# One decode step with attention over a cache: where the last rows of W_up lie, how wq is transferred, and which queue brings the first K tile

## The chip, the core and the metric

The kernel runs on one core of a Trainium2 chip. The core has a matrix engine (TensorE, PE), a vector engine (VectorE, DVE), a scalar engine (ScalarE, ACT), a general engine (GpSimd, POOL) and an engine that here only issues transfers (SyncE, SP). Transfers from memory are issued by SP and by ScalarE, each on a queue of its own (q1 and q10 in the profile), and are carried out by the core's 16 DMA engines. Data lies in SBUF (128 partitions); matrix products land in PSUM. The metric is the device time of one execution in microseconds (us); lower is better.

## The reference

One token goes through two branches that a sigmoid gate mixes. Branch a is attention of 16 query heads over 8 cached key and value heads of 65536 positions; branch b is a small gated network.

```python
g = _sigmoid((x * gate_w).sum(-1, keepdims=True))
a = _A_ref(x, A_k_cache, A_v_cache, A_wq, A_wo)   # q = x @ wq; softmax(q k^T / 16) v; @ wo
b = _B_ref(x, B_W_gate, B_W_up, B_W_down)         # (relu(x W_gate) * (x W_up)) @ W_down
return g * a + (1 - g) * b
```

Everything is bf16. x has 448 elements, wq is 448 x 4096, wo 4096 x 448, W_gate and W_up are 448 x 1792, W_down is 1792 x 448. The caches are 8 x 65536 x 256 each, 268 MB each, and each is read once.

## The kernel before

K and V stream through a ring of three SBUF buffers, `ring[0..2]`, each of 128 partitions x 64 KB. A tile of K or V (4 for each of the 8 heads, 32 of each) fills one buffer. A list `order` (lines 228 to 244) fixes the order of the tiles and of wo's two parts on SP's queue and assigns each tile the next buffer in turn; `held` and `freed` (lines 254 to 259) say which operations must have read a buffer before the next tile may be issued into it. For a K tile DVE transposes the buffer in place in 32 x 32 blocks (line 454), PE forms the scores (`f_qk`), DVE takes their maximum and ScalarE the exponential. When all four tiles of a head are done, the weights are rescaled and V tiles are multiplied (`make_pv`).

Every operation is entered into a plan with an engine, a key (its place in that engine's order, no time) and the operations it depends on. `_Plan.finish` sorts each engine's operations by key and puts semaphore waits where a dependency needs one; `mop` marks the operations on the shared PSUM bank `M_ps`, and `serialize` puts these one behind another in the order of keys.

The start is the part that the change touches. The buffers `ring[1]` and `ring[2]` first hold weights, and `ring[0]` gets the first K tile, K0.

- ScalarE issues W_gate's first 384 rows (3 rows to a partition), x, gate_w, W_gate's last 64 rows as half rows on 128 partitions (`wfh[0]`), and W_up's first 384 rows (lines 271 to 277).
- SP issues wq's first 384 rows (`wq3`, one transfer of 128 partitions, into `ring[2]`), wq's last 64 rows (`wqa`, into `ring[1]`), W_up's last 64 rows as half rows (`wfh[1]`), K0, then W_down, which waits for the query projection because it overwrites `wq3`, and then K1 into `ring[1]`, which waits for the query projection as well (`held[1]` is `["q"]`). K2 goes into `ring[2]` and waits for the gate, up and down products.
- When x is there, POOL spreads its last 64 elements (`f_xp`), PE turns x into columns (`f_xT`), DVE copies them to `xT` and lays them out for the query projection (`f_xw`). The sigmoid of the gate is computed along the way (`z0` to `z7`, over POOL, DVE, ScalarE and PE).
- PE then runs the query projection (`f_q`, 48 matmuls in a loop; `f_q2`, 16), the gate and up products (`f_gu` over 384 rows, 24 matmuls; `f_gu2` over the last 64 rows, 8), and, when DVE has formed h (lines 656 to 660), the down product (`f_dn`).

In a loop made by `step`, the addresses are held in registers of PE's sequencer, which are moved on in each turn. `raw_mm` takes a matmul with or without a load of its weights; `same_weights` is a matmul that uses the weights loaded before it. A matmul of one output row uses 32 columns of the array, so four stand side by side in four column groups.

At the end, wo for heads 0 to 3 and the rest of wo come behind the V tiles, and the products of PE's `f_wo` add up in the PSUM bank `A_ps`, into which the down product has gone already.

Of the kernel before, what the change touches and what calls it, by code (L numbers as in the profile page):

```python
# [9 lines left out]
U32 = mybir.dt.uint32  # L10
# [15 lines left out]
class _Plan:  # L26
# [8 lines left out]
    def op(self, eng, key, fn, deps=(), incs=1, split=False):  # L35
        o = _Op(eng, key, fn, deps, incs=incs, split=split)
        self.ops.append(o)
        return o

    def dma(self, eng, key, sem, fn, deps=()):  # L40
        if sem not in self.dsem:
            self.dsem[sem] = self.es.enter_context(self.nc.semaphore("d_" + sem))
        o = _Op(eng, key, fn, deps, dma=sem)
        self.ops.append(o)
        return o
# [66 lines left out]
def bass_gated_mix__gqa_block_cached__glu_gated_reglu__decode_kernel(  # L112
# [25 lines left out]
    NR3 = R3 * 128  # L138
    HD = D // 2
    NW = R3 + 2  # L140
    NX = R3 + 2
    FT = F // 128
    SCALE = 1.0 / 16.0
    NEGBIG = -3.0e38
# [7 lines left out]
    with es:  # L152
# [40 lines left out]
        g_row = P2[1][:, 1024:1024 + 2 * FW].bitcast(F32)  # L193
        h_row = P2[1][:, 0:FW]

        wq3 = ring[2][:, 0:R3 * NQ]
        wqa = ring[1][:, 0:NQ // 2]
        WB = R3 * NQ
        wf3 = [ring[2][:, WB + i * R3 * F:WB + (i + 1) * R3 * F] for i in range(2)]
        WB += 2 * R3 * F  # L200
        wfh = [ring[2][:, WB + i * (F // 2):WB + (i + 1) * (F // 2)] for i in range(2)]
        assert WB + F <= U * DH and FW * 4 == F and FW <= 512
        wd_sb = ring[2][:, 0:FT * D].rearrange("p (ft d) -> p ft d", ft=FT)

        ST = [ps("ST%d" % i, [128, 512], F32) for i in range(2)]
# [45 lines left out]
        T_END = t + 20.0  # L251


        slot, held, freed = {}, {1: ["q"], 2: ["gu", "dn"]}, {}
        r = 0
        for kind, i, _ in order:
            if kind in ("k", "v"):
# [6 lines left out]
        for key, (kind, i, _) in home.items():  # L264
# [7 lines left out]
            wf3[0], B_W_gate[0:NR3, :].rearrange("(p k) f -> p (k f)", k=R3)))  # L272
        d_x = dma("ac", -9, "x", lambda e: e.dma_start(x_row, A_x[0, :, :]))
        d_gw = dma("ac", -8, "gw", lambda e: e.dma_start(gw_row, gate_w.rearrange("(o d) -> o d", o=1)))
        half = lambda i, W: lambda e: e.dma_start(wfh[i], W[NR3:D, :].rearrange("r (c f) -> (r c) f", c=2))
        d_wh0 = dma("ac", -7, "wfh0", half(0, B_W_gate))
        d_wu = dma("ac", -6, "wf1", lambda e: e.dma_start(
            wf3[1], B_W_up[0:NR3, :].rearrange("(p k) f -> p (k f)", k=R3)))

        c_xp = op("gp", -0.3, lambda e: e.memset(x_per, 0.0))  # L280
        c_o1 = op("gp", -0.2, lambda e: e.memset(one_t[:], 1.0))
        c_nil = op("gp", -0.1, lambda e: e.memset(nil_t[:], 0.0))
# [37 lines left out]
        def f_xT(e):  # L320
            for kt in range(R3):
                e.matmul(XT_ps[:, kt:kt + 1], x_row[0:1, kt:NR3:R3], one_t[0:1, 0:1], start=True, stop=True)
            for kt in range(NX - R3):
                ins = e.matmul(XT_ps[:, R3 + kt:R3 + kt + 1], x_per[0:1, kt * 128:kt * 128 + 128], one_t[0:1, 0:1], start=True, stop=True)  # L324
            return ins

        def f_xp(e):
            xr = x_row[0:1, NR3:D]
            for c in range(2):
                ins = e.tensor_copy(x_per[0:1, 129 * c:129 * c + 127:2], xr)  # L330
            return ins
        x0_ = op("gp", 0.97, f_xp, [d_x, c_xp])
        x1_ = mop("pe", 0.98, f_xT, [d_x, c_o1, x0_])

        def f_xT2(e):
            return e.tensor_copy(xT[:], XT_ps)  # L336
        x2_ = mop("dv", 0.985, f_xT2, [x1_])
        g_em = op("dv", 2.1, lambda e: e.tensor_reduce(
            emat[:], identb[:].rearrange("p (y r) -> p r y", r=8)[:, 0:4, :], AX.X, ALU.max), [g_idb])
# [67 lines left out]
        def step(e, ws, vs, dw, dv, count, mms):  # L407
            rw, rv = pr[0:len(ws)], pr[len(ws):len(ws) + len(vs)]
            w0 = at(ws[0], True)

            def body():
                e.reg_alu(rw[0], rw[0], dw, ALU.add)
                adds(e, (rw[0], ws[0], True), [(r_, w, True) for r_, w in zip(rw[1:], ws[1:])])
                e.reg_alu(rv[0], rv[0], dv, ALU.add)
                adds(e, (rv[0], vs[0]), [(r_, v, False) for r_, v in zip(rv[1:], vs[1:])])
                for o, i, j, pos, size in mms:
                    ins = raw_mm(e, o, via(ws[i], rw[i]), via(vs[j], rv[j]), pos, True, size)
                return ins
            v0 = at(vs[0])
            return rolled(e, [(rw[0], w0 - dw), (rv[0], v0 - dv)], rv[0], v0 + (count - 1) * dv, body)  # L420
# [190 lines left out]

        for kind, i, t in issue:
            if kind == "wq":
                l_["wq"] = dma("sp", t, "wq", lambda e: e.dma_start(wq3, A_wq[0:NR3, :].rearrange("(p k) n -> p (k n)", k=R3)))
                l_["wqh"] = dma("sp", t + 0.01, "wqh", lambda e: e.dma_start(
                    wqa, A_wq[NR3:D, :].rearrange("r (c n) -> (r c) n", c=2)))
                d_wh1 = dma("sp", t + 0.02, "wfh1", half(1, B_W_up))
                tq = tL["wq", 0]
                l_["qm"] = mop("pe", tq, f_q, [l_["wq"], q0, c_nil, g_idb], incs=J)
                l_["q"] = mop("pe", tq + 8, f_q2, [l_["qm"], l_["wqh"]], incs=J // 2)  # L620
# [5 lines left out]
            elif kind == "gu":  # L626
                t = tL["gu", 0]
                a1 = [d_wg, d_wu]
                a2 = [d_wh0, d_wh1]

                def f_gu(e):
                    for kt in range(R3):
                        for i_ in range(2):
                            for w in range(4):
                                o, v = OP[i_][32 * w:32 * w + 1, 0:FW], wf3[i_][:, kt * F + w * FW:kt * F + (w + 1) * FW]
                                if i_ == 0:
                                    ins = e.matmul(o, xT[:, kt:kt + 1], v, start=(kt == 0), stop=False, skip_group_check=True,
                                                   tile_position=(0, 32 * w))
                                else:
                                    ins = same_weights(e, o, xT[:, kt:kt + 1], v, kt == 0, (0, 32 * w))  # L640
                    return ins

                def f_gu2(e):
                    for w in range(4):
                        for i_ in range(2):
                            o, v = OP[i_][32 * w:32 * w + 1, 0:FW], wfh[i_][:, w % 2 * FW:(w % 2 + 1) * FW]
                            x = xT[:, R3 + w // 2:R3 + w // 2 + 1]
                            if i_ == 0:
                                e.matmul(o, x, v, start=False, stop=False, skip_group_check=True, tile_position=(0, 32 * w))
                            else:  # L650
                                ins = same_weights(e, o, x, v, False, (0, 32 * w))
                    return ins
                tg, tr0 = tL["k", 0] - 6.6, tL["k", 0] - 0.5
                l_["gm"] = op("pe", tL["gu", 0] + 3, f_gu, a1 + [x2_, c_ps[3]])
                l_["gu"] = op("pe", tr0, f_gu2, a2 + [l_["gm"]])
                l_["relu"] = op("dv", tr0 + 0.1, lambda e: e.tensor_scalar_max(g_row, OP[0][:, 0:FW], 0.0), [l_["gu"], z1, l_["xm"]])
                l_["h"] = op("dv", tr0 + 0.2, lambda e: e.scalar_tensor_tensor(
                    h_row.rearrange("p (t q) -> p q t", q=32), g_row.rearrange("p (q t) -> p q t", q=32), gb[:, 1:2],
                    OP[1][:, 0:FW].rearrange("p (q t) -> p q t", q=32), ALU.mult, ALU.mult), [l_["relu"], z7])
                l_["hT"] = op("dv", tr0 + 0.3, lambda e: e.transpose(h_row, h_row), [l_["h"]])  # L660
            elif kind == "wd":
                a3 = dma("sp", t, "wd", lambda e: e.dma_start(wd_sb, B_W_down.rearrange("(p ft) d -> p ft d", ft=FT)), [l_["q"]])

                def f_dn(e):
                    f_nil(e, [A_ps])
# [3 lines left out]
            elif kind == "k":  # L669
                n = i  # L670
                h, t_ = divmod(n, NTH)
                sl = slot["k", n]
                kd = dma("sp", t, "r%d" % sl, lambda e, n=n, sl=sl: e.dma_start(ring[sl][:], k_src(n)), free(("k", n)))
# [89 lines left out]

        t7 = last["tn", H - 1]
        for i in range(len(WOP)):
            for k, (h, lo, hi) in enumerate(WOP[i]):
                key = tL["wo", i] + 0.01 * k
                if i == 1:
                    key = t7 + (-0.3 if h < NP else 0.6) + 0.01 * k
                wv = wo_sb[:, h:h + 2, :, :].rearrange("p h s n -> p (h s) n") if h < NP else wo_sb[:, h, :, :]  # L770

                def f_wo(e, h=h, lo=lo, hi=hi, wv=wv, end=(i == 1 and k == len(WOP[i]) - 1), roll=(i == 0)):
                    if roll:
                        return step(e, [attnT[:, h * 4 + lo:h * 4 + lo + 1]], [wv[:, lo, g * HD:(g + 1) * HD] for g in range(2)], 2, 2 * D, hi - lo,
                                    [(A_ps[32 * g:32 * g + 1, 0:HD], 0, g, (0, 32 * g), (128, 32)) for g in range(2)])
                    for s in range(lo, hi):
                        for g in range(2):
                            c = h * 4 + s
                            ins = e.matmul(A_ps[32 * g:32 * g + 1, 0:HD], attnT[:, c:c + 1], wv[:, s, g * HD:(g + 1) * HD],
                                           start=False, stop=(end and s == hi - 1), skip_group_check=True,  # L780
                                           tile_position=(0, 32 * g))
                    return ins
                fin = op("pe", key, f_wo, [l_["wo", h, lo], last["norm", h], last["norm", h + 1] if h < NP else None], incs=hi - lo if i == 0 else 1)
        f1 = [op(("dv", "ac")[g], T_END, lambda e, g=g: (e.copy if g else e.tensor_copy)(
            fin_o[:, g * HD:(g + 1) * HD], A_ps[32 * g:32 * g + 1, 0:HD]), [fin]) for g in range(2)]
        f2 = dma("ac", T_END + 1, "out", lambda e: e.dma_start(
# [38 lines left out]
```

## Time and profile before

| | us |
|---|---|
| median of three runs | 1275.67 (1275.54 to 1275.78) |
| the profiled execution | 1275.64 |
| its span, from the first to the last instruction | 1274.2 |
| DVE busy | 648.7 (51% of the span) |
| PE busy | 371.4 (29%) |
| ScalarE busy | 58.2 (5%) |
| POOL busy | 37.2 (3%) |
| moved by the DMA engines | 549.20 MB, 431 GB/s in the mean |

A row of the timeline reads: start in us from the beginning of the span, duration in us, engine, line of the kernel, operation, the tile written and the tiles read, their sizes, and how many instructions were merged into the row; in brackets the idle time of that engine before it and what ended it. SPq and ACTq are the issuing of transfers by those engines. A row of the table by stretches gives the stretch, its length, each engine's busy time and (in brackets) its instructions, the granted PE clock as a share of full speed, the mean busy share of the 16 DMA engines and the rate in GB/s. Transfers are counted where their packets start, so that in stretches of a few us a share can exceed 1. A DMA queue's row gives packets, MB, and the time of its packets as a share of 16 engines over the span.

### The profile page before, as it was taken

What the parts mean: (1) busy time and instruction counts of PE and PEld (TensorE: products, weight loads), DVE (VectorE), ACT (ScalarE), POOL (GpSimd) and SP (SyncE); (2) the same over time, 40 slices, a digit from 0 to 9 for tenths busy, and PEclk for the clock granted to TensorE, in tenths of its full rate; (3) what the DMA queues carried; (4) which work ended last, traced back from release to release, by engine and by line L of the source; (5) the groups of instructions that cost most, each with busy time, mean ns of one, the idle gap of its engine ahead of it and who ended that gap; (6) DMA issues with size and microseconds to landing.
All of it is one profiled execution on the core that took longest, in us unless ns stands there. A gap on an engine that the chain in (4) does not pass through costs nothing.

```text
span 1274.2 us, 9555 instructions
## 1 busy us (share of the span) xinstructions
PE 371.4 (29%) x4483; PEld 105.0 (8%) x2909; DVE 648.7 (51%) x171; ACT 58.2 (5%) x112; POOL 37.2 (3%) x94
## 2 busy tenths in 40 slices
PE   4413222323133331224220342311332203223154
PEld 2101000101000000001000010000100000000010
DVE  1797633566534655445555454556535565336511
ACT  0000000000000000000000000000000000000000
POOL 2000000000000100001000010000100001000010
PEclk9566666656666665665656676556766556666577
DMA  9999999999999999999999999999999999999998
GB/s 414 429 444 428 426 428 430 447 438 428 428 432 428 442 435 434 428 434 428 441 434 434 428 434 430 439 434 434 428 438 428 436 434 434 430 438 428 436 421 378
DMA packets 11522, 549.20 MB, mean 431 GB/s; under 512 B 1267, under 2 KB 1654, under 8 KB 2422
## 3 DMA queue, kind: packets, MB, share of 16 engines
q1 hardware_dynamic: 11072, 546.05, 99.2%
q10 hardware_dynamic: 438, 2.98, 0.6%
q8 instruction: 8, 0.13, 0.0%
q14 instruction: 4, 0.03, 0.0%
HBM read 549.03 MB, written 0.00 MB: 431 GB/s over the span
## 4 chain that ended last, share of the span: by engine, by line
DMA 42%; DVE 32%; PE 16%; another core or an unknown queue 7%; issue 1%; POOL 0%; ACT 0%; SPq 0%; ACTq 0%
DMA ring<-in_A_k_cache_dram 34%; DVE ring L454 27%; PE ST L373 9%; PE O L373 5%; DMA ring<-in_A_v_cache_dram 4%; DMA ring<-in_A_wo_dram 3%; DVE P L701 1%; DVE P L699 1%; PE M_ps L373 1%; DVE o_sb L497 1%; DMA P<-in_A_x_dram 1%; DVE nmb L680 1%; PE ST L403 0%; PE M_ps L694 0%
## 5 line engine op out<-in xcount | busy, mean ns | idle before, releaser
L454 DVE STREAM_TRANSPOSE ring<-ring 128x16384 uint32<-128x16384 uint32 (+1 forms) x36 | 552.3, 15345 | 318.9 <-DMA ring<-in_A_k_cache_dram 318.9
L403 PE MATMUL ST<-nil_t,identb 1*128 1x1 bf16 x32 | 5.1, 158 | 767.6 <-DVE ring L454 767.6
L373 PE MATMUL ST<-ring,xm 128*16 x2048 | 185.2, 537 | 4.6 <-issue 0.7
L373 PE MATMUL O<-ring,P 128*32 x2016 | 133.9, 425 | 20.8 <-DMA ring<-in_A_v_cache_dram 18.3
L680 DVE TENSOR_REDUCE nmb<-ST 128x1 f32<-128x512 f32 x32 | 22.0, 688 | 185.0 <-PE ST L373 185.0
L682 ACT ACTIVATE P<-ST,nmb 128x512 bf16<-128x512 f32 x32 | 45.2, 1413 | 1082.8 <-DVE nmb L680 1082.8
L373 PEld LDWEIGHTS ST<-ring,xm 128*16 x2048 | 61.5, 112 | 115.2 <-issue 101.5
L403 PEld LDWEIGHTS ST<-nil_t,identb 1*128 1x128 bf16 x32 | 3.2, 100 | 792.6 <-issue 792.6
L497 DVE CAST_PREDICATED o_sb<-bm,O 128x512 bf16<-128x512 uint16 (+1 forms) x33 | 22.3, 679 | 69.2 <-PE O L356 46.9
L690 POOL TENSOR_TENSOR hs<-selc,hs 128x2 f32<-128x2 f32 x8 | 1.6, 196 | 1143.7 <-DVE hs L688 1143.7
L373 PEld LDWEIGHTS O<-ring,P 128*32 x504 | 15.7, 113 | 112.9 <-issue 110.4
L699 DVE TENSOR_TENSOR P<-P,hs 128x2048 bf16<-128x2048 bf16 x8 | 18.3, 2292 | 8.1 <-ACT hs L696 8.1
L702 POOL TENSOR_TENSOR hs<-hs,rs 128x4 f32<-128x4 f32 x8 | 18.4, 2305 | 13.6 <-ACT hs L696 13.6
L701 DVE STREAM_TRANSPOSE P<-P 128x2048 bf16<-128x2048 bf16 x8 | 18.5, 2311 | 0.3
L707 PE MATMUL M_ps<-hs,ones_f 128*128 128x2 f32 x16 | 4.7, 364 | 30.3 <-POOL hs L706 30.3
L373 PE MATMUL M_ps<-ring,P 128*128 x64 | 13.0, 341 | 1.5 <-PE M_ps L373 0.3
L525 PE MATMUL M_ps<-emat,o_sb 128*64 128x2 bf16 x48 | 3.0, 185 | 22.0 <-ACT o_sb L507 22.0
L682 ACT ACTIVATION_READ_ACCUMULATOR P<-ST,nmb 128x1 f32 x32 | 8.4, 263 | 0.0
L373 PEld LDWEIGHTS M_ps<-ring,P 128*128 x64 | 7.5, 119 | 6.9 <-issue 5.3
L336 DVE CAST xT<-M_ps 128x5 bf16<-128x5 f32 x1 | 0.2, 167 | 14.7 <-PE M_ps L324 14.7
L622 DVE STREAM_TRANSPOSE P<-P 128x128 uint32<-128x128 uint32 x1 | 0.3, 311 | 12.7 <-ACT P L621 12.7
L707 PEld LDWEIGHTS M_ps<-hs,ones_f 128*128 128x128 f32 x16 | 4.0, 312 | 30.9 <-POOL hs L706 30.9
(103 smaller groups left out, 94.0 us busy)
## 6 DMA issues: line engine op xcount, KB each, us to landing
ring<-in_A_v_cache_dram SPq DMA_DIRECT2D x3, 4096.0 KB, 28.9
ring<-in_A_v_cache_dram SPq DMA_DIRECT2D x2, 2048.0 KB, 36.3
ring<-in_A_wq_dram SPq DMA_DIRECT2D x1, 3072.0 KB, 13.2
ring<-in_A_wo_dram SPq DMA_DIRECT2D x1, 1792.0 KB, 19.6
ring<-in_B_W_down_dram SPq DMA_DIRECT2D x1, 1568.0 KB, 10.1
ring<-in_B_W_gate_dram ACTq DMA_DIRECT2D x1, 1344.0 KB, 13.4
ring<-in_B_W_up_dram ACTq DMA_DIRECT2D x1, 1344.0 KB, 26.5
ring<-in_A_wo_dram SPq DMA_DIRECT2D x1, 896.0 KB, 40.3
```

The costliest lines, as they stand in the source:

```text
L373: return e.add_instruction(mybir.InstMatmult(name=nc.get_next_instruction_name(), engine=e.engine, ins=[v, w], outs=[e.lower_ap(o)], start ...
L403: e.matmul(o, identb[0:1, :], nil_t[0:1, 0:1], start=True, stop=False, skip_group_check=True)
L454: return lambda e: e.transpose(v, v)
L497: return e.copy_predicated(dst, m.to_broadcast(list(src.shape)), src)
L525: ins = e.matmul(T_ps[p0:p0 + 64, s:c1 + 1:c1 - s], t[:, c:c + 64], emat2[:], start=(s == 0), stop=False, skip_group_check=True, tile_posi ...
L680: smax[n] = op("dv", tk + 26, lambda e, n=n, NM=NM, t_=t_: e.tensor_reduce(NM[:, t_:t_ + 1], ST[n % 2][:], AX.X, ALU.max, negate=True), [q ...
L682: aexp[n] = op("ac", tk + 27, lambda e, n=n, t_=t_, NM=NM, RS=RS, Ph=Ph: e.activation(Ph[:, t_:2048:4], ST[n % 2][:], ACTF.Exp, bias=NM[:, ...
L690: h2 = op("gp", T + 13.55, lambda e, X=X: e.tensor_tensor(X[:, 2:4], selc[:, 2:4], X[:, 0:1].to_broadcast([128, 2]), ALU.mult), [h1, g_sel])
L699: rsc = op("dv", T + 16, lambda e, X=X, pb=pb: e.tensor_tensor(pb, pb, X[:, 12:16].unsqueeze(1).to_broadcast([128, 512, 4]), ALU.mult), [h ...
L701: last["ev", h] = [op("dv", T + 17, lambda e, Ph=Ph: e.transpose(Ph[:], Ph[:]), [rsc])]
L702: l0 = op("gp", T + 18, lambda e, X=X, RS=RS: e.tensor_tensor(X[:, 16:20], X[:, 12:16], RS[:], ALU.mult), [h7])
L707: l3 = mop("pe", T + 19, lambda e, X=X: e.matmul(LS_ps, ones_f[:, :], X[:, 6:8], start=True, stop=True), [l2, c_one])
```

## The change

W_up's last 64 rows are split: 36 rows go onto six partitions (0, 4, 8, ... 20), six whole rows to each (`wue`), and 28 rows go as quarter rows onto 112 partitions (`wuq`). To multiply these, x's elements are laid out to match: `xe` has for each of the six rows a column over 32 partitions with zeros between, `xq` has for each quarter a column over 112. These come out of four copies on POOL in place of two, fifteen matmuls in `f_xT` in place of five, and two extra copies from PSUM by ScalarE. The 32 partitions of `wue` are cleared by DVE first, and SP's transfer waits for that. `f_gu2` then has 4 matmuls for W_gate's last rows, 4 for the quarter rows and 24 for the six rows, each with its own load of weights.

wq's first 384 rows are issued as eight transfers of 16 partitions, every eighth one. They now lie in `ring[1]` together with wq's last rows, so that W_down, in `ring[2]`, overwrites nothing and waits for nothing; W_gate's and W_up's places in `ring[2]` move with it. SP issues W_down ahead of K1 as before, but K0 is issued by ScalarE behind its other weights. K1 waits for the gate and up products as well as for the query projection. `f_gu` becomes a loop of three turns behind two matmuls that set its banks, ordered behind the query projection. In `f_wo`, heads 0 to 3 become one loop in place of two.

```diff
-    NX = R3 + 2
+    NE, RE, NQR = 6, 6, 4
+    NX = R3 + 2 + RE + NQR
...
-        wq3 = ring[2][:, 0:R3 * NQ]
-        wqa = ring[1][:, 0:NQ // 2]
-        WB = R3 * NQ
+        wq3 = ring[1][:, 0:R3 * NQ]
+        wqa = ring[1][:, R3 * NQ:R3 * NQ + NQ // 2]
+        WB = FT * D
...
-        slot, held, freed = {}, {1: ["q"], 2: ["gu", "dn"]}, {}
+        slot, held, freed = {}, {1: ["q", "gu"], 2: ["gu", "dn"]}, {}
...
+        c_wue = op("dv", -0.4, lambda e: e.memset(wue.bitcast(U32), 0))
+        c_xe = op("gp", -0.35, lambda e: e.memset(xe, 0.0))
+        c_xq = op("gp", -0.34, lambda e: e.memset(xq, 0.0))
...
-            for kt in range(NX - R3):
-                ins = e.matmul(XT_ps[:, R3 + kt:R3 + kt + 1], x_per[0:1, kt * 128:kt * 128 + 128], one_t[0:1, 0:1], start=True, stop=True)
+            for kt in range(2):
+                e.matmul(XT_ps[:, R3 + kt:R3 + kt + 1], x_per[0:1, kt * 128:kt * 128 + 128], one_t[0:1, 0:1], start=True, stop=True)
+            for j in range(RE):
+                e.matmul(XT_ps[0:32, R3 + 2 + j:R3 + 3 + j], xe[0:1, j * 32:(j + 1) * 32], one_t[0:1, 0:1], start=True, stop=True)
+            for w in range(NQR):
+                c = R3 + 2 + RE + w
+                ins = e.matmul(XT_ps[0:KQ, c:c + 1], xq[0:1, w * KQ:(w + 1) * KQ], one_t[0:1, 0:1], start=True, stop=True)
...
+        x2e = mop("ac", 0.983, lambda e: e.copy(xT[0:32, R3 + 2:R3 + 2 + RE], XT_ps[0:32, R3 + 2:R3 + 2 + RE]), [x1_])
+        x2e = mop("ac", 0.984, lambda e: e.copy(xT[0:KQ, R3 + 2 + RE:], XT_ps[0:KQ, R3 + 2 + RE:]), [x1_])
...
-                l_["wq"] = dma("sp", t, "wq", lambda e: e.dma_start(wq3, A_wq[0:NR3, :].rearrange("(p k) n -> p (k n)", k=R3)))
+                wqs = A_wq[0:NR3, :].rearrange("(a b k) n -> a b (k n)", b=8, k=R3)
+                for b in range(8):
+                    l_["wq"] = dma("sp", t + 0.001 * b, "wq", lambda e, b=b: e.dma_start(wq3[b:128:8, :], wqs[:, b, :]))
...
-                d_wh1 = dma("sp", t + 0.02, "wfh1", half(1, B_W_up))
+                d_wh1 = dma("sp", t + 0.02, "wue", lambda e: e.dma_start(
+                    wue[0:4 * NE - 3:4, :], B_W_up[NR3:E0, :].rearrange("(p j) f -> p (j f)", j=RE)), [c_wue])
+                d_wuq = dma("ac", -6.5, "wuq", lambda e: e.dma_start(wuq, B_W_up[E0:D, :].rearrange("r (c f) -> (r c) f", c=NQR)))
...
                 def f_gu(e):
-                    for kt in range(R3):
...
+                    f_nil(e, OP[0:2])
+                    return step(e, [xT[:, 0:1]], [wf3[i_][:, w * FW:(w + 1) * FW] for i_ in range(2) for w in range(4)], 2, 2 * F, R3,
+                                [(OP[i_][32 * w:32 * w + 1, 0:FW], 0, 4 * i_ + w, (0, 32 * w), (128, 32), i_ == 0) for i_ in range(2) for w in range(4)])
...
+                    for j in range(RE):
+                        for w in range(4):
+                            ins = e.matmul(OP[1][32 * w:32 * w + 1, 0:FW], xT[0:32, R3 + 2 + j:R3 + 3 + j], wue[:, j * F + w * FW:j * F + (w + 1) * FW],
+                                           start=False, stop=False, skip_group_check=True, tile_position=(0, 32 * w))
...
-                l_["gm"] = op("pe", tL["gu", 0] + 3, f_gu, a1 + [x2_, c_ps[3]])
-                l_["gu"] = op("pe", tr0, f_gu2, a2 + [l_["gm"]])
+                l_["gm"] = op("pe", tL["gu", 0] + 3, f_gu, a1 + [x2_, c_ps[3], l_["qm"]], incs=R3)
+                l_["gu"] = op("pe", tr0, f_gu2, a2 + [l_["gm"], x2e])
...
-                a3 = dma("sp", t, "wd", lambda e: e.dma_start(wd_sb, B_W_down.rearrange("(p ft) d -> p ft d", ft=FT)), [l_["q"]])
+                a3 = dma("sp", t, "wd", lambda e: e.dma_start(wd_sb, B_W_down.rearrange("(p ft) d -> p ft d", ft=FT)))
...
-                kd = dma("sp", t, "r%d" % sl, lambda e, n=n, sl=sl: e.dma_start(ring[sl][:], k_src(n)), free(("k", n)))
+                kd = dma("sp" if n else "ac", t if n else -5, "r%d" % sl if n else "k0", lambda e, n=n, sl=sl: e.dma_start(ring[sl][:], k_src(n)), free(("k", n)))
...
-            for k, (h, lo, hi) in enumerate(WOP[i]):
+            for k, (h, lo, hi) in enumerate([(0, 0, 8 * len(WOP[0]))] if i == 0 else WOP[i]):
```

More of the change, by code (lines that the diff above doesn't have):

```diff
@@ L194, in bass_gated_mix__gqa_block_cached__glu_gated_reglu__decode_kernel @@
         h_row = P2[1][:, 0:FW]
-        wq3 = ring[2][:, 0:R3 * NQ]
-        wqa = ring[1][:, 0:NQ // 2]
-        WB = R3 * NQ
+        wq3 = ring[1][:, 0:R3 * NQ]
+        wqa = ring[1][:, R3 * NQ:R3 * NQ + NQ // 2]
+        WB = FT * D
         wf3 = [ring[2][:, WB + i * R3 * F:WB + (i + 1) * R3 * F] for i in range(2)]
         WB += 2 * R3 * F
-        wfh = [ring[2][:, WB + i * (F // 2):WB + (i + 1) * (F // 2)] for i in range(2)]
-        assert WB + F <= U * DH and FW * 4 == F and FW <= 512
+        wgh = ring[2][:, WB:WB + F // 2]
+        WB += F // 2
+        E0 = NR3 + NE * RE
+        KQ = NQR * (D - E0)
+        wue = ring[2][0:32, WB:WB + RE * F]
+        WB += RE * F
+        wuq = ring[2][0:KQ, WB:WB + FW]
+        xe = P2[0][0:1, 1056:1056 + 32 * RE]
+        xq = P2[1][0:1, 448:448 + NQR * (KQ + 1)]
+        assert 448 >= max(D, FW) and 448 + NQR * (KQ + 1) <= 1024 and 32 * RE <= 256 and 4 * NE <= 32 and KQ <= 128
+        assert WB + FW <= U * DH and FW * 4 == F and FW <= 512
         wd_sb = ring[2][:, 0:FT * D].rearrange("p (ft d) -> p ft d", ft=FT)
@@ L274, in bass_gated_mix__gqa_block_cached__glu_gated_reglu__decode_kernel @@
         d_gw = dma("ac", -8, "gw", lambda e: e.dma_start(gw_row, gate_w.rearrange("(o d) -> o d", o=1)))
-        half = lambda i, W: lambda e: e.dma_start(wfh[i], W[NR3:D, :].rearrange("r (c f) -> (r c) f", c=2))
-        d_wh0 = dma("ac", -7, "wfh0", half(0, B_W_gate))
+        d_wh0 = dma("ac", -7, "wgh", lambda e: e.dma_start(wgh, B_W_gate[NR3:D, :].rearrange("r (c f) -> (r c) f", c=2)))
         d_wu = dma("ac", -6, "wf1", lambda e: e.dma_start(
             wf3[1], B_W_up[0:NR3, :].rearrange("(p k) f -> p (k f)", k=R3)))
+        c_wue = op("dv", -0.4, lambda e: e.memset(wue.bitcast(U32), 0))
+        c_xe = op("gp", -0.35, lambda e: e.memset(xe, 0.0))
+        c_xq = op("gp", -0.34, lambda e: e.memset(xq, 0.0))
         c_xp = op("gp", -0.3, lambda e: e.memset(x_per, 0.0))
@@ L329, in f_xp @@
             for c in range(2):
-                ins = e.tensor_copy(x_per[0:1, 129 * c:129 * c + 127:2], xr)
-            return ins
-        x0_ = op("gp", 0.97, f_xp, [d_x, c_xp])
+                e.tensor_copy(x_per[0:1, 129 * c:129 * c + 127:2], xr)
+            e.tensor_copy(xe.rearrange("o (j p) -> o j p", p=32)[:, :, 0:4 * NE - 3:4], x_row[0:1, NR3:E0].rearrange("o (i j) -> o j i", j=RE))
+            return e.tensor_copy(xq.rearrange("o (w z) -> o w z", w=NQR)[:, :, 0:KQ - 3:4], x_row[0:1, E0:D].unsqueeze(1).to_broadcast([1, NQR, D - E0]))
+        x0_ = op("gp", 0.97, f_xp, [d_x, c_xp, c_xe, c_xq])
         x1_ = mop("pe", 0.98, f_xT, [d_x, c_o1, x0_])
         def f_xT2(e):
-            return e.tensor_copy(xT[:], XT_ps)
+            return e.tensor_copy(xT[:, 0:R3 + 2], XT_ps[:, 0:R3 + 2])
+        x2e = mop("ac", 0.983, lambda e: e.copy(xT[0:32, R3 + 2:R3 + 2 + RE], XT_ps[0:32, R3 + 2:R3 + 2 + RE]), [x1_])
+        x2e = mop("ac", 0.984, lambda e: e.copy(xT[0:KQ, R3 + 2 + RE:], XT_ps[0:KQ, R3 + 2 + RE:]), [x1_])
         x2_ = mop("dv", 0.985, f_xT2, [x1_])
@@ L415, in body @@
                 adds(e, (rv[0], vs[0]), [(r_, v, False) for r_, v in zip(rv[1:], vs[1:])])
-                for o, i, j, pos, size in mms:
-                    ins = raw_mm(e, o, via(ws[i], rw[i]), via(vs[j], rv[j]), pos, True, size)
+                for o, i, j, pos, size, *load in mms:
+                    ins = raw_mm(e, o, via(ws[i], rw[i]), via(vs[j], rv[j]), pos, load != [False], size)
                 return ins
@@ L628, in bass_gated_mix__gqa_block_cached__glu_gated_reglu__decode_kernel @@
                 a1 = [d_wg, d_wu]
-                a2 = [d_wh0, d_wh1]
+                a2 = [d_wh0, d_wh1, d_wuq]
                 def f_gu(e):
-                    for kt in range(R3):
[L633 to L641, printed above, removed]
+                    f_nil(e, OP[0:2])
+                    return step(e, [xT[:, 0:1]], [wf3[i_][:, w * FW:(w + 1) * FW] for i_ in range(2) for w in range(4)], 2, 2 * F, R3,
+                                [(OP[i_][32 * w:32 * w + 1, 0:FW], 0, 4 * i_ + w, (0, 32 * w), (128, 32), i_ == 0) for i_ in range(2) for w in range(4)])
@@ L643, in f_gu2 @@
                 def f_gu2(e):
                     for w in range(4):
[L645 to L651, printed above, removed]
+                        e.matmul(OP[0][32 * w:32 * w + 1, 0:FW], xT[:, R3 + w // 2:R3 + w // 2 + 1], wgh[:, w % 2 * FW:(w % 2 + 1) * FW],
+                                 start=False, stop=False, skip_group_check=True, tile_position=(0, 32 * w))
@@ new lines, in f_gu2 @@
+                    for w in range(4):
+                        c = R3 + 2 + RE + w
+                        e.matmul(OP[1][32 * w:32 * w + 1, 0:FW], xT[0:KQ, c:c + 1], wuq,
+                                 start=False, stop=False, skip_group_check=True, tile_position=(0, 32 * w))
+                    for j in range(RE):
+                        for w in range(4):
+                            ins = e.matmul(OP[1][32 * w:32 * w + 1, 0:FW], xT[0:32, R3 + 2 + j:R3 + 3 + j], wue[:, j * F + w * FW:j * F + (w + 1) * FW],
+                                           start=False, stop=False, skip_group_check=True, tile_position=(0, 32 * w))
@@ L769, in bass_gated_mix__gqa_block_cached__glu_gated_reglu__decode_kernel @@
                     key = t7 + (-0.3 if h < NP else 0.6) + 0.01 * k
-                wv = wo_sb[:, h:h + 2, :, :].rearrange("p h s n -> p (h s) n") if h < NP else wo_sb[:, h, :, :]
+                wv = wo_sb[:, h:NP, :, :].rearrange("p h s n -> p (h s) n") if h < NP else wo_sb[:, h, :, :]
                 def f_wo(e, h=h, lo=lo, hi=hi, wv=wv, end=(i == 1 and k == len(WOP[i]) - 1), roll=(i == 0)):
@@ L782, in f_wo @@
                     return ins
-                fin = op("pe", key, f_wo, [l_["wo", h, lo], last["norm", h], last["norm", h + 1] if h < NP else None], incs=hi - lo if i == 0 else 1)
+                fin = op("pe", key, f_wo, [l_["wo", h, lo], last["norm", h], last["norm", h + max(1, (hi - lo) // 4 - 1)] if h < NP else None], incs=hi - lo if i == 0 else 1)
         f1 = [op(("dv", "ac")[g], T_END, lambda e, g=g: (e.copy if g else e.tensor_copy)(
```

## The prediction

> **What bounds the kernel now.** I read the page's head and its DMA queues first, because the slices show the DMA row full from end to end.
>
> ```profile
> span 1274.2 us, 9555 instructions
> ...
> q1 hardware_dynamic: 11072, 546.05, 99.2%
> q10 hardware_dynamic: 438, 2.98, 0.6%
> q8 instruction: 8, 0.13, 0.0%
> ```
>
> The two hardware queues hold the 16 DMA engines for 99.2 + 0.6 = 99.8% of the span. All idle time together is about 0.2%, 2.5 us. The rate is 546.05 MB in 0.992 x 1274.2 = 1264 us: 432 GB/s, 27.0 GB/s for one engine. Next the stretches of the run:
>
> ```profile
> core 0: us, PE busy (x) PEld busy (x) DVE busy (x) ACT busy (x) POOL busy (x), PEclk, DMA share, GB/s
> 0.00:2.00 2.00, 0.00 (x0) 0.00 (x0) 0.00 (x0) 0.00 (x0) 1.47 (x9) 1.00 0.47 111
> 2.00:4.00 2.00, 0.00 (x0) 0.00 (x0) 0.00 (x0) 1.03 (x1) 1.60 (x8) 1.00 0.71 270
> 4.00:6.00 2.00, 0.00 (x0) 0.00 (x0) 0.00 (x0) 0.26 (x1) 1.55 (x7) 1.00 0.90 386
> 18.00:24.00 6.00, 5.84 (x31) 4.24 (x31) 2.19 (x8) 0.00 (x0) 0.00 (x0) 1.00 1.30 560
> 24.00:26.00 2.00, 2.00 (x20) 1.67 (x17) 0.00 (x0) 0.00 (x0) 0.00 (x0) 1.00 0.32 136
> 42.00:640.00 598.00, 170.50 (x2090) 48.08 (x1406) 333.12 (x73) 28.07 (x51) 13.92 (x28) 0.62 1.00 433
> 640.00:1238.00 598.00, 164.76 (x2099) 44.89 (x1319) 302.29 (x71) 25.80 (x49) 13.91 (x28) 0.63 1.00 433
> 1238.00:1272.00 34.00, 17.89 (x181) 2.89 (x87) 3.60 (x8) 0.00 (x0) 0.00 (x0) 0.69 0.96 406
> ```
>
> From 42 to 1238 us the share is 1.00: nothing in the loop over heads waits for compute in a way that costs time. The bytes do not change, so the change can act only in the first 42 us, in how evenly the 16 engines are loaded, or by opening a gap. In the first 6 us the deficit against 432 GB/s is 2 x (321 + 162 + 46) = 1058 KB, 2.45 us.
>
> **The chain at the start**, from the timeline and the DMA issues, decides whether a gap opens.
>
> ```profile
> 0.74 0.38 SPq L614 DMA_DIRECT2D ring<-in_A_wq_dram  x1
> 13.88 0.42 POOL L330 COPY P<-P 1x64 bf16<-1x64 bf16 x2 [4.28 <-DMA P<-in_A_x_dram]
> 14.36 0.24 PE L322 MATMUL M_ps<-one_t,P 1*128 1x1 bf16 x3 [14.36 <-POOL P L330]
> 14.46 0.19 PE L324 MATMUL M_ps<-one_t,P 1*128 1x1 bf16 x2
> 14.68 0.17 DVE L336 CAST xT<-M_ps 128x5 bf16<-128x5 f32 x1 [14.68 <-PE M_ps L324]
> 17.88 0.16 PE L403 MATMUL M_ps<-nil_t,identb 1*128 1x1 bf16 x1 [0.34 <-DVE gb L317]
> 18.20 7.94 PE L373 MATMUL M_ps<-ring,P 128*128 x48 [0.15 <-issue]
> 32.65 0.33 SPq L662 DMA_DIRECT2D ring<-in_B_W_down_dram  x1
> 33.71 0.59 PE L356 MATMUL O<-ring,xT 128*1 128x448 bf16 x4
> 34.08 0.59 PE L637 MATMUL O<-ring,xT 128*1 128x448 bf16 x4
> 36.92 0.62 DVE L656 TENSOR_SCALAR P<-O 128x448 f32<-128x448 f32 x1 [3.15 <-PE O L356]
> 40.33 17.26 DVE L454 STREAM_TRANSPOSE ring<-ring 128x8192 uint32<-128x8192 uint32 x2
> 62.09 8.71 DVE L454 STREAM_TRANSPOSE ring<-ring 128x8192 uint32<-128x8192 uint32 x1 [4.51 <-DMA ring<-in_A_k_cache_dram]
> ...
> ring<-in_A_wq_dram SPq DMA_DIRECT2D x1, 3072.0 KB, 13.2
> ...
> ring<-in_B_W_down_dram SPq DMA_DIRECT2D x1, 1568.0 KB, 10.1
> ```
>
> SP issues W_down at 32.65, when the query projection is done, and K1 right behind. W_down lands 10.1 us later, at 42.75. It is the last work ahead of K1, so the engines run dry of everything before K1 at about 42.7, and K1 was queued nine microseconds earlier.
>
> **The change part by part.**
>
> *W_down ahead of K0, K0 on ScalarE's queue.* The same bytes stand ahead of K1, so the dry point stays at 42.7; only K0 and W_down change places. K0 now lands last, at about 42.7. Its two transposes began at 40.33, 3.4 us after the relu (36.92), and with the gate and up products done at 40.8 (below) they begin at 44.2. They take 17.26 us and end at 61.5; K1's start at 62.09, after 4.51 us idle, which hides this with 0.6 us to spare.
>
> ```profile
> L673 SPq DMA_DIRECT2D ring<-in_A_k_cache_dram x32: 327/328/585, 2.1 to 1134.9; - x32
> ...
> DMA to landing us min/median/max: 29.1/49.8/51.0
> ```
>
> Beyond that lies the queue: a tile of 8.39 MB takes 19.4 us at 432 GB/s, and the shortest of 32 K issues stood 29.1 us ahead of its landing, so every tile has at least 9.7 us in hand. K2, which waits for the down product behind h, and K3, which waits for K0's scores, leave 2 to 4 us later out of that; without it they would cost those 2 to 4. ScalarE issues seven transfers, two more than before (0.3 to 0.4 us each, as SP's above); its first compute comes after x, so this is free. SP issues W_down without the wait for the query projection: a wait gone, and queued behind it only K1.
>
> *K1 now waits for "gu" too* (the list of what holds ring slot 1). This is the risky part: the wait on PE moves from the end of the query projection to the end of the gate and up products, and all K and V tiles are queued behind it on SP. Before, "gu" ended at 36.92 (the relu's start). Added ahead of it:
> - POOL: two more copies at 0.21 (two in 0.42): 0.4.
> - PE: ten more one-column matmuls for x; five took 14.36 to 14.65, 0.06 each: 0.6.
> - ACT: two small PSUM copies that DVE's copy of xT must follow, as the ops on the shared bank are put in series. The nearest row is DVE's own, 0.17: 0.4 with hand-overs. Together 1.4.
> - f_gu as a loop: a nil matmul and the loop's start, 17.88 to 18.20: 0.3. Its 24 matmuls stay.
> - f_gu2: 32 matmuls for 8. Four run side by side and a group of four starts each 0.37 us (33.71, 34.08), so six more groups: 2.2.
>
> K1's issue: 36.92 + 1.4 + 0.3 + 2.2 = 40.8. The lower bound takes the fast rate of PE throughout: 31 matmuls in 6 us, then 20 in 2, so the projection's 48 could take 4.8 instead of 7.94, giving 37.7. All slow they take 9.3, giving 42.2.
>
> ```profile
> 1212.44 2.29 DVE L699 TENSOR_TENSOR P<-P,hs 128x2048 bf16<-128x2048 bf16 x1 [0.99 <-ACT hs L696]
> 1212.48 2.30 POOL L702 TENSOR_TENSOR hs<-hs,rs 128x4 f32<-128x4 f32 x1 [1.68 <-ACT hs L696]
> 1217.15 0.33 DVE L585 MEMSET o_sb<- 128x320 uint32 x1
> 1217.21 0.20 POOL L709 TENSOR_TENSOR hs<-hs,gb 128x2 f32<-128x2 f32 x1 [1.60 <-DVE hs L708]
> 1267.91 0.82 PE L555 MATMUL O<-ring,P 128*4 128x512 bf16 x12 [0.26 <-DMA ring<-in_A_v_cache_dram]
> 1273.05 0.27 ACTq L786 DMA_DIRECT2D out_dram<-P  x1
> ```
>
> How soon does an issue become data? The output's transfer is issued at 1273.05 and the span ends at 1274.2: at most 1.15 us. So K1 flows at 41.95, before 42.7. No gap, by 0.75 us; with the upper bound a gap of 0.65.
>
> *The memset of W_up's 32 partitions* on DVE: 5376 words at 0.33 us per 320: 5.5 us. DVE's first work was at 14.68, so it is hidden. A DVE operation can hold POOL up (2.30 us for four elements beside the tensor_tensor), but beside a memset of words POOL took its ordinary 0.20. SP waits for the memset before the six-partition transfer and W_down, until about 6 us; the queue holds wq until about 14 (0.74 + 13.2). Free. POOL's two memsets of one row lie in its idle time before 13.88.
>
> *wq by eight transfers.* Same bytes. SP's issue costs about 0.4 us each, so the last leaves at 0.74 + 7 x 0.38 = 3.4; one brings 24 KB to each engine, 0.91 us at 27.0 GB/s, so issuing keeps ahead. The possible gain is an earlier start of all engines: of the 2.45 us lost by 6 us, 0.74 + 1.15 pass before anything can flow, so between 0 and 0.6 can be won. I take 0.3, the middle, as no row separates the engines.
>
> *W_up's last 64 rows.* Before, 229 KB over all engines: 14.3 KB each, 0.53 us. After, 28 rows as quarters: 6.3 KB each, 0.23; and 36 rows on six partitions, 21.5 KB each, 0.80. If six partitions go to six engines, those get +0.50 and ten get -0.30. The queue q8 carried eight instruction refills of 16 KB, 0.6 us each at 27.0 GB/s, each on some engine; the view does not say which. If the ten are the late ones the end moves by -0.30, if the six are, by +0.50. I take -0.2, nearer the first, as most engines get less. [...]
>
> *One loop for wo's first four heads*: PE then has the DMA of V to wait for; free, and it saves one loop start off the path.
>
> **Sum.** Against the profiled execution (1274.2 span, 1275.64 in all, 0.03 under the runs' median of 1275.67): start -0.3, balance -0.2, gap +0.1 (a fifth of 0.65, since it needs the upper bound): -0.4. From the median: 1275.3.
>
> **Rivals.** 0.2% is 2.55 us, about what a measurement of this kernel can tell from no change; so 1273.1 and 1278.2 are the limits.
> 1. *The start and the balance come in full* (-0.6, -0.3, and the tail follows): 1274.4, with luck 1273.8. For it: the deficit is there. Against: the other queue's gate transfer still goes out as one. To pass 1273.1 there is no place in the profile.
> 2. *The six partitions are late, or K1 leaves a small gap*: +0.50 or +0.65, at most both and no start gain: 1276.2 to 1277.2. For it: the margin is only 0.75.
> 3. *K1 comes much too late* (the other side): if the 24 matmuls over 32 partitions do not run four side by side, each takes 0.37 instead of 0.09, 6.7 us more; K1 leaves at 47.5, flows at 48.6, and the gap is 5.9: 1281.6. It decides above 0.2% once the gap passes 2.6, that is with K1's issue after 44.1. Against it: with a load each, 12 matmuls of 512 columns took 0.82 us at the end, 0.07 each.
> 4. *The pieces of wq each drain the engines*: seven more boundaries at up to 1.15 us, 8 us: 1283.3. Against it: across dozens of transfers the share is 1.00. [...]
>
> **How the numbers follow.** Forecast as summed, between 1274.6 and 1275.9: 0.56. Rival 1: 0.14, of which 0.03 under 1273.1. Rival 2, to 1278.2: 0.19. Rival 3: 0.09. Rival 4: 0.02. Faster 0.03, slower 0.11, same 0.86. The range 1274.1 to 1277.4 leaves out rivals 3 and 4 and the ends of 1 and 2.
>
> **What would show it.** DMA share 1.00 around 42 us, K1's issue near 41, W_down landed long before, DVE's K0 transposes from about 44, K1's transposes still near 62, the first 6 us at a higher rate. I am wrong if a window around 42 us shows the DMA well under its rate, or if the share between 42 and 1238 falls: then a wait that I took as hidden is not.

## The result and the profile after

The changed kernel takes 1283.86 us (median of 6 runs, 1283.55 to 1284.28) against 1275.76 for the kernel before in the same comparison (1275.54 to 1275.90): a ratio of 1.0063, 95% interval 1.0053 to 1.0074. It is 8.1 us slower, and the whole interval lies above 1. The profiled span grew from 1274.2 to 1282.1 us.

The head and the DMA queues of the changed kernel's page:

```profile
span 1282.1 us, 9655 instructions
...
q1 hardware_dynamic: 10908, 537.56, 97.5%
q10 hardware_dynamic: 710, 11.47, 2.2%
```

K0's 8.39 MB have moved from q1 to q10. Together the two queues hold the DMA engines for 99.7% of the span, as before (99.8%), yet the same 549.20 MB took 7.9 us longer. So the engines did not stand idle for the missing time: they were busy and moved less. A share of busy time does not say that; the rate beside it does. The stretches show where, first of the kernel before, then of the changed one (the last two columns are DMA share and GB/s):

```profile
6.00:10.00 4.00, 0.00 (x0) 0.00 (x0) 0.00 (x0) 0.00 (x0) 2.94 (x12) 1.00 0.99 427
10.00:20.00 10.00, 2.83 (x17) 2.08 (x18) 3.34 (x11) 0.20 (x1) 1.79 (x5) 1.00 1.11 466
20.00:30.00 10.00, 8.72 (x51) 5.55 (x49) 0.35 (x4) 0.00 (x0) 0.00 (x0) 1.00 0.98 423
```

```profile
6.00:10.00 4.00, 0.00 (x0) 0.00 (x0) 0.45 (x1) 0.00 (x0) 3.19 (x14) 1.00 1.05 241
10.00:20.00 10.00, 1.58 (x17) 1.38 (x17) 3.70 (x13) 0.41 (x3) 2.57 (x8) 1.00 1.02 221
20.00:30.00 10.00, 7.27 (x42) 5.28 (x43) 0.00 (x0) 0.00 (x0) 0.00 (x0) 1.00 0.98 387
30.00:42.00 12.00, 9.92 (x65) 2.96 (x53) 0.59 (x2) 2.49 (x9) 0.00 (x0) 0.72 1.00 430
50.00:640.00 590.00, 168.73 (x2079) 48.26 (x1397) 334.61 (x73) 28.08 (x51) 13.92 (x28) 0.62 1.00 433
```

From 6 to 20 us, while wq's eight transfers pass, the rate is about half of 433 GB/s at a share above 1. The deficit against 433 from 6 to 30 us is 4 x 192 + 10 x 212 + 10 x 46 = 3348 KB, 7.7 us: nearly the whole loss. From 30 us on the rate is that of full transfers again (430, then 433). The timeline and the DMA issues of the changed kernel show what followed:

```profile
0.74 5.29 SPq L636 DMA_DIRECT2D ring<-in_A_wq_dram  x8
10.37 0.42 POOL L347 COPY P<-P 1x64 bf16<-1x64 bf16 x2 [0.15 <-DMA P<-in_A_x_dram]
22.61 0.18 PE L423 MATMUL M_ps<-nil_t,identb 1*128 1x1 bf16 x1 [7.11 <-DMA ring<-in_A_wq_dram]
41.09 0.54 PE L662 MATMUL O<-ring,xT 128*1 128x448 bf16 x4 [0.15 <-PE O L393]
43.36 11.09 SPq L693 DMA_DIRECT2D ring<-in_A_k_cache_dram  x2
43.36 0.62 DVE L676 TENSOR_SCALAR P<-O 128x448 f32<-128x448 f32 x1 [4.69 <-PE O L670]
55.46 17.30 DVE L474 STREAM_TRANSPOSE ring<-ring 128x8192 uint32<-128x8192 uint32 x2 [8.61 <-DMA ring<-in_A_k_cache_dram]
```

x was there 3.5 us earlier than before (10.37 against 13.88), but the query projection stood 7.11 us for wq and began at 22.61 in place of 17.88. K1 left at 43.36, as its wait for the gate and up products had it. That could look like the cause, but K0 was itself late and its transposes began only at 55.46, so the queue still held work when K1 joined it.

### The profile page after: what moved, and what is told of

It reads as the page before. It is cut to its first block, busy times and chain, and to the rows that moved or that the text cites. A ratio compares the mean times of both kernels' runs of the same rounds, so it can differ in the third digit from the quotient of the medians.

```text
span 1282.1 us, 9655 instructions
## 1 busy us (share of the span) xinstructions
PE 376.1 (29%) x4519; PEld 107.1 (8%) x2948; DVE 653.1 (51%) x172; ACT 58.4 (5%) x114; POOL 38.4 (3%) x98
## 2 busy tenths in 40 slices
DMA packets 11630, 549.20 MB, mean 428 GB/s; under 512 B 1385, under 2 KB 1756, under 8 KB 2524
## 4 chain that ended last, share of the span: by engine, by line
DMA 39%; DVE 34%; PE 16%; another core or an unknown queue 9%; issue 1%; SPq 0%; ACT 0%; POOL 0%
DMA ring<-in_A_k_cache_dram 30%; DVE ring L474 30%; PE ST L393 9%; PE O L393 5%; DMA ring<-in_A_v_cache_dram 4%; DMA ring<-in_A_wo_dram 3%; DMA ring<-in_A_wq_dram 1%; DVE o_sb L517 1%; DVE P L721 1%; DVE P L719 1%; PE M_ps L393 1%; DVE nmb L700 1%; SPq L636 0%; PE ST L423 0%
```

## The experiments

### One part undone, one part alone

First, wq in one transfer again, in the changed kernel:

```diff
-                wqs = A_wq[0:NR3, :].rearrange("(a b k) n -> a b (k n)", b=8, k=R3)
-                for b in range(8):
-                    l_["wq"] = dma("sp", t + 0.001 * b, "wq", lambda e, b=b: e.dma_start(wq3[b:128:8, :], wqs[:, b, :]))
+                l_["wq"] = dma("sp", t, "wq", lambda e: e.dma_start(wq3, A_wq[0:NR3, :].rearrange("(p k) n -> p (k n)", k=R3)))
```

> The changed kernel with wq's 384 rows in one transfer again. Four theories for the 8.1 us, and for the 221 GB/s from 10 to 20 us at a DMA share of 1.02. Ports: sixteen partitions eight apart reach only half of the ways into SBUF, so wq runs at half rate. Pieces: each of the eight transfers costs something. Memory: rows read 196 KB apart are slow at the source. These three expect 1275.3 (1274.5 to 1276.5) here, and 430 GB/s from 10 to 20 us. Wait: K1 leaves late, at 43.4 in place of 33.0, because it waits for the gate and up products; that expects 1283 to 1284 still.

Measured: 1276.12 us (11 runs) beside 1275.80 of before, ratio 1.0004, interval 0.9995 to 1.0013: no difference that can be told. The loss is gone with this one edit, though K1 still waits for the gate and up products. Stretches and timeline of this run:

```profile
0.00:2.00 2.00, 0.00 (x0) 0.00 (x0) 0.09 (x1) 0.00 (x0) 1.47 (x10) 1.00 0.74 172
2.00:4.00 2.00, 0.00 (x0) 0.00 (x0) 2.00 (x1) 0.00 (x0) 1.72 (x7) 1.00 0.52 191
4.00:6.00 2.00, 0.00 (x0) 0.00 (x0) 2.00 (x1) 1.28 (x1) 1.59 (x6) 1.00 0.94 404
10.00:20.00 10.00, 2.12 (x20) 1.76 (x21) 1.87 (x7) 0.41 (x3) 2.40 (x8) 1.00 1.01 419
...
39.87 9.60 SPq L691 DMA_DIRECT2D ring<-in_A_k_cache_dram  x2
43.28 17.28 DVE L474 STREAM_TRANSPOSE ring<-ring 128x8192 uint32<-128x8192 uint32 x2
62.60 8.71 DVE L474 STREAM_TRANSPOSE ring<-ring 128x8192 uint32<-128x8192 uint32 x1 [2.04 <-DMA ring<-in_A_k_cache_dram]
```

From 10 to 20 us the rate is 419 GB/s. K1 left at 39.87; DVE stood 2.04 us before K1's transposes, so the later start of K0's transposes was hidden. The wait theory falls.

Then the other way round: in the kernel before, wq's single transfer was replaced by the changed kernel's eight, and nothing else.

```diff
-                l_["wq"] = dma("sp", t, "wq", lambda e: e.dma_start(wq3, ...
+                wqs = A_wq[0:NR3, :].rearrange("(a b k) n -> a b (k n)", b=8, k=R3)
+                for b in range(8):
+                    l_["wq"] = dma("sp", t + 0.001 * b, "wq", lambda e, b=b: e.dma_start(wq3[b:128:8, :], wqs[:, b, :]))
```

> The kernel before with one part of the change alone: wq in eight transfers of every eighth partition, all else as before (K1 waits for the query projection only, W_down behind K0). Ports, pieces and memory: 7 to 8 us slower than before, 1282.5 to 1284. Wait: 1275.8.

Measured: 1283.83 us, ratio 1.0063 (1.0048 to 1.0079): the whole change's loss, within 0.03 us, at half rate again.

```profile
10.00:20.00 10.00, 0.87 (x7) 0.70 (x7) 3.69 (x13) 0.20 (x1) 1.83 (x5) 1.00 0.94 209
```

So this part alone makes the loss, with or without the other parts.

### Pieces, source or destination

The same eight pieces with other neighbours:

```diff
-                wqs = A_wq[0:NR3, :].rearrange("(a b k) n -> a b (k n)", b=8, k=R3)
+                wqs = A_wq[0:NR3, :].rearrange("(b a k) n -> b a (k n)", b=8, k=R3)
...
-... e.dma_start(wq3[b:128:8, :], wqs[:, b, :]))
+... e.dma_start(wq3[16 * b:16 * b + 16, :], wqs[b]))
```

> The changed kernel with wq still in eight transfers of 16 partitions, but of neighbours (0 to 15, 16 to 31, ...), so that each reads one contiguous 393 KB. Ports: 16 neighbours reach fewer ways than 16 spread ones. [...] A quarter of 433 GB/s is 108: 3.15 MB take 29 us in place of 14.5, so 1298 (1293 to 1302). Pieces: 1283.9 as the changed kernel. Memory: 1276, as the source is contiguous. Wait: 1283.9.

Measured: 1296.41 us, ratio 1.0163 (1.0148 to 1.0179). Eight pieces as before, but 12.6 us slower still, although each piece now reads one contiguous block. Its stretches:

```profile
10.00:20.00 10.00, 0.00 (x0) 0.00 (x0) 0.00 (x0) 0.00 (x0) 0.19 (x1) 1.00 1.14 165
20.00:30.00 10.00, 1.58 (x17) 1.38 (x17) 3.69 (x13) 0.41 (x3) 2.35 (x7) 1.00 0.97 115
34.00:42.00 8.00, 6.81 (x49) 5.37 (x49) 0.00 (x0) 0.00 (x0) 0.00 (x0) 1.00 1.03 414
```

From 20 to 30 us, where almost only wq is left, the rate is 115 GB/s, a little over a quarter of 433 (108); the quarter in the ports theory's 1298 was the author's assumption, with no row behind it ahead of this run. Nearly the full rate (414) is back by 34 to 42. The pieces theory expected no difference from the changed kernel, the memory theory a gain; both fall here. The other half of the crossing keeps the destinations of the changed kernel and reads contiguous blocks (`wq3[b:128:8, :]` from `wqs[b]` of the second arrangement):

> The changed kernel with wq written to every eighth partition as in it, but read in contiguous blocks of 393 KB. The rows of wq then lie on other partitions than the query projection takes them for, so q is another one; the work is the same. Ports: 1283.9 (1283 to 1285), as the destinations are the same. Pieces: 1283.9. Memory: 1276. Wait: 1283.9.

Measured: 1283.77 us, ratio 1.0063 (1.0047 to 1.0078), and 221 GB/s from 10 to 20 us, as in the changed kernel.

```profile
10.00:20.00 10.00, 1.58 (x17) 1.39 (x17) 3.69 (x13) 0.41 (x3) 2.54 (x8) 1.00 1.01 221
```

With the same destinations, how the source is read makes no difference; with eight pieces of the same size either way, which partitions are written makes all of it. The traces' records of single packets say the same in time. A packet of wq is one partition's 24 KB; its median was 0.91 us in the kernel before, 1.76 in the changed kernel, 1.77 in this run and 3.00 with 16 neighbours. So the engines were busy with the same packets for longer.

### Which sets of partitions are slow

A way is a word of the ports theory, for whatever several partitions share on the path from the DMA engines into SBUF; no run shows one. What the runs show is the rate for each set of partitions. Two more spacings of 16 partitions are set against two readings, plain fours and distance. The edit changes only the slices: for a step s of 2 or 4, piece b writes `wq3[16*s*c + r : 16*s*(c+1) : s]` with c, r = divmod(b, s).

> The changed kernel with wq in eight transfers of 16 partitions that lie two apart (0, 2, ... 30, and so on). [...] Plain fours: each four neighbours have a way of their own, 32 in all, and fewer than 16 of them cost; then eight apart would have reached 16, which the changed kernel's half rate speaks against, and this one reaches 8: 1283.9. Distance: the closer the partitions, the slower; between neighbours (1296.4) and eight apart (1283.9), so about 1290 to 1293.

> The changed kernel with wq in eight transfers of 16 partitions that lie four apart (0, 4, ... 60, and so on). [...] Plain fours: 16 ways, 1276.1. Distance: between two apart and eight apart, about 1287.

Measured: two apart 1284.27 us (ratio 1.0064, 1.0047 to 1.0081), four apart 1283.40 us (1.0059, 1.0043 to 1.0076). From 10 to 20 us the one moves

```profile
10.00:20.00 10.00, 1.58 (x17) 1.38 (x17) 3.69 (x13) 0.41 (x3) 2.54 (x8) 1.00 0.99 211
```

and the other

```profile
10.00:20.00 10.00, 1.58 (x17) 1.38 (x17) 3.54 (x13) 0.41 (x3) 2.48 (x8) 1.00 1.00 218
```

Two, four and eight apart all run at half rate (211, 218 and 221 GB/s against 433). Distance expected a graded answer and plain fours expected four apart to be free; both fall. What is left is the measured grouping: about half the rate for 16 partitions two, four or eight apart, about a quarter (115 GB/s) for 16 neighbours. Why it falls that way was not shown.

Then larger pieces. Four transfers of 32 partitions and two of 64:

```diff
-                wqs = ... b=8, k=R3)
-                for b in range(8): ... wq3[b:128:8, :]
+                wqs = ... b=4, k=R3)
+                for b in range(4): ... wq3[b:128:4, :]
```

> The changed kernel with wq in four transfers of 32 partitions, every fourth one. The runs before left the ports theory alone: 16 spread partitions ran at half rate wherever they were read from, 16 neighbours at a quarter, one transfer of 128 at the full rate. Two forms of it are open. Reach: what counts is how many ways a whole transfer reaches; 32 partitions four apart reach them all, so 1276.1 (1275.3 to 1277). Moment: what counts is which ways the 16 DMA engines write at one time; if an engine takes two partitions in a row of the list (0 and 4, 8 and 12, ...), the 16 engines are first at 0, 8, 16, ... and then at 4, 12, 20, ..., each time on half of the ways as in the changed kernel, so 1283.9 (1282 to 1285).

> The changed kernel with wq in two transfers of 64 partitions, every second one. Reach: all ways, 1276.1 (1275.3 to 1277). [...]

Measured: 1275.81 us (ratio 0.9999, 0.9989 to 1.0009) and 1275.77 us (0.9998, 0.9988 to 1.0008). Neither differs from the kernel before, as the form "reach" expected. The form "moment" falls only with the division that it assumed, in which each engine takes its partitions in a row of the list. How the engines divide the list among themselves wasn't observed, so with another division it stays open.

One rival was not run: that a transfer of 16 partitions, as many rows as there are engines, is slow by itself. Such a rule doesn't explain why 16 neighbours run at half the rate of 16 spread ones (115 GB/s and 221). It has no place either for what the packets of the K tile's eighths (next section) show: they took 5.1 us each, but 4.7 in the median around the passage from the fourth piece to the fifth. Why they were shorter there was not shown.

The run with every fourth partition:

```profile
0.00:2.00 2.00, 0.00 (x0) 0.00 (x0) 0.09 (x1) 0.00 (x0) 1.47 (x10) 1.00 0.38 54
2.00:4.00 2.00, 0.00 (x0) 0.00 (x0) 2.00 (x1) 0.00 (x0) 1.72 (x7) 1.00 0.73 274
4.00:6.00 2.00, 0.00 (x0) 0.00 (x0) 2.00 (x1) 1.28 (x1) 1.59 (x6) 1.00 1.11 471
10.00:20.00 10.00, 6.14 (x45) 4.74 (x46) 3.52 (x13) 0.41 (x3) 2.35 (x8) 1.00 0.97 407
...
35.92 9.59 SPq L693 DMA_DIRECT2D ring<-in_A_k_cache_dram  x2
```

The query projection was done sooner and K1 left at 35.92, four microseconds before the run with one transfer, and the time is the same: the DMA queue had work either way. Neither version beats the kernel before.

### The same thing away from the start

In the kernel before, one K tile in the middle of the run is split:

```diff
-                kd = dma("sp", t, "r%d" % sl, lambda e, n=n, sl=sl: e.dma_start(ring[sl][:], k_src(n)), free(("k", n)))
+                NB_ = 8 if n == 16 else 1
+                for b in range(NB_):
+                    kd = dma("sp", t + 0.001 * b, "r%d" % sl, lambda e, n=n, sl=sl, b=b, NB_=NB_: e.dma_start(
+                        ring[sl][b:128:NB_, :], k_src(n)[b:128:NB_, :]), free(("k", n)))
```

> The kernel before, with one K tile in the middle (the first of head 4) in eight transfers of every eighth partition; all else as before. If half of the ways is the whole cause, it holds anywhere: 8.39 MB at half of 433 GB/s take 19.4 us longer, and nothing stands in the queue that could use the other half: 1295.2 (1293 to 1297). If the loss belongs to the start (first transfers, two queues, small pieces beside others), 1275.9.

> The same tile in four transfers of every fourth partition, which reach all ways: 1275.9 (1275.3 to 1276.5). If splitting a large tile costs by itself, more.

Measured: in eighths 1299.22 us (1298.24 to 1305.33; ratio 1.0195, 1.0167 to 1.0223), in fourths 1275.73 us (ratio 1.0000, 0.9990 to 1.0009). Stretches of the run in eighths:

```profile
540.00:580.00 40.00, 9.79 (x137) 2.85 (x89) 22.42 (x8) 2.16 (x5) 0.00 (x0) 0.63 1.01 439
580.00:640.00 60.00, 12.08 (x138) 3.44 (x87) 20.44 (x8) 1.85 (x4) 3.47 (x7) 0.61 1.00 264
588.00:628.00 40.00, 8.81 (x113) 2.21 (x50) 5.79 (x6) 1.85 (x4) 3.47 (x7) 0.67 1.00 210
640.00:680.00 40.00, 9.94 (x129) 2.59 (x81) 19.53 (x3) 1.43 (x2) 0.00 (x0) 0.59 1.01 435
```

and of the run in fourths:

```profile
588.00:628.00 40.00, 14.29 (x170) 4.17 (x115) 23.03 (x7) 1.85 (x4) 3.47 (x7) 0.69 1.01 437
```

The loss is not tied to the start. It is larger than expected: 23.5 us in place of 19.4, above the expected range. The deficit of the 60 us is 60 x 169 = 10.1 MB, 23.4 us, so all of it lies in this stretch. The packet records show how it adds up. A packet of 64 KB took 2.42 us in the kernel before and 5.11 us in the split tile, 2.11 times as long and not twice: 128 packets on 16 engines, eight for each in the mean, make 8 x 2.69 = 21.5 us. The rest lies at the edges. 146 packets took over 3 us and the tile has 128, so packets of the tiles ahead and behind were slowed as well; all extra packet time together, divided by 16 engines, is 23.4 us. Why a packet takes more than twice as long wasn't settled.

## Why the prediction was wrong

**The step that failed** is "wq by eight transfers", with "Same bytes" as its price: one transfer "brings 24 KB to each engine, 0.91 us at 27.0 GB/s, so issuing keeps ahead". That carries the rate of one engine from transfers over all 128 partitions to transfers over 16. No row showed a large transfer on so few partitions, and the step was not bounded from above. The runs show that the rate goes with the set of partitions that a transfer writes: 433 GB/s for all 128, about half of it for the three spread sets of 16 (211, 218 and 221), about a quarter for 16 neighbours (115). The term stood in the sum with its gain alone, -0.3, and measured +8.0 (the part alone, 1283.83 against 1275.80).

**Rival 4** named this step and came near in size (1283.3), with a chance of 0.02, but by another mechanism: pieces that "each drain the engines". The share of 1.02 shows engines that are not drained, and four or two pieces of wq cost nothing. Its agreement in time is an accident.

**W_down ahead of K0: "the dry point stays at 42.7".** It rests on the same wrong rate. Without the slow wq it held: with one transfer, K0's last packet ended at 42.74 us, and K1's first had begun at 41.60. In the changed kernel these were 52.56 and 46.76, so there was no gap either, only everything later.

**K1's wait for the gate and up products.** The issue was put at 40.8; with one transfer it was 39.87, within the bounds. In the changed kernel it was 43.36, over the upper bound of 42.2, because that bound did not have wq's landing in it. The rest of that chain was well sized: K0's transposes were put at 44.2 to 61.5 and ran from 43.28 for 17.28 us with one transfer. The 24 matmuls over 32 partitions were put at 2.2 us and took 1.37 in the changed kernel, so rival 3's row of matmuls one after another did not come about.

```profile
41.94 1.37 PE L670 MATMUL O<-ring,xT 32*1 32x448 bf16 x24
```

The stretches around K1 in the run with one transfer:

```profile
38.00:42.00 4.00, 1.82 (x32) 0.43 (x24) 2.09 (x2) 0.00 (x0) 0.00 (x0) 0.93 0.93 393
42.00:46.00 4.00, 2.28 (x13) 0.62 (x13) 3.97 (x3) 0.00 (x0) 0.00 (x0) 0.50 0.92 393
46.00:60.00 14.00, 2.80 (x16) 0.70 (x16) 14.00 (x2) 0.00 (x0) 0.00 (x0) 0.50 1.04 449
```

Packets count where they start, and what 38 to 46 lacks against 433 (8 x 40 = 320 KB) stands in 46 to 60 above it (14 x 16 = 224 KB) for the most part, so no gap of more than a few tenths of a us is there.

**The start.** Of the 0.6 us at most, 0.3 was taken. Against 433 GB/s the first 6 us lost 2 x (261 + 242 + 29) = 1064 KB with one transfer, as many as in the kernel before (1058 against 432), and 2 x (379 + 159 - 38) = 1000 KB with four pieces: at best 0.15 us, and the times show none. The pieces did not bring wq sooner to the engines: its first packet began at 1.74 us with one transfer, at 4.99 in the changed kernel and at 5.31 with four pieces, while W_gate's packets had the engines. Why it began later wasn't settled.

**The balance of W_up's last rows** was put at -0.2 between -0.30 and +0.50. With one transfer the whole rest of the change stands at a ratio of 1.0004 (0.9995 to 1.0013), 0.3 us on the slow side with an interval that holds zero. Neither end can be excluded by it, and the part was not measured alone. In that run the six packets of 21.5 KB took 0.80 us each, as estimated, and all six ran at one time, from 14.64 to 15.98 us, which fits six engines, though no record names them; what that costs at the end is not shown.

**The memset** was hidden, as expected (4.54 us measured, 5.5 expected, and done long before wq).

## What to carry to other kernels

When a transfer is cut by partitions, ask of each piece which partitions it writes: here every eighth, fourth or second partition in groups of 16 about halved the rate (221, 218 and 211 of 433 GB/s), and 16 neighbours cut it to about a quarter (115), while every fourth partition in groups of 32 cost nothing (1275.81 us beside 1275.90). A rate read from full transfers is no price for a transfer of another shape. And a DMA share of 1.00 is no proof of full speed (it stood at 1.00 with 210 GB/s in the split K tile): read the GB/s beside it.

## What the runs showed of the hardware that was not expected

- DMA engines that are held back count as busy: the share was 1.02 at 221 GB/s and 1.00 at 210, as each packet's time grew (24 KB in 1.76 us in place of 0.91).
- The loss isn't repaid by transfers of the other queue. In the kernel before with wq alone changed, W_up's first rows were issued on ScalarE's queue at 2.57 us, but the trace has no packet of theirs between 8 and 16 us, while wq's pass at half rate; the whole loss stayed. Why they did not flow meanwhile is open.
- Pieces that write every second, fourth or eighth partition are dear to issue on SP: eight of 16 partitions took 5.21 to 5.29 us, 0.65 to 0.66 each, and the K tile's eight 5.02, with no transfer of ScalarE near them; eight of 16 neighbours took 3.77, 0.47 each, and the one of 128 partitions 0.38. It cost no time that these runs show.
